# Opening of a Fourier-mixing and gated-MLP kernel: the norm row kept in its own tile, loads and weight folds in another order

## The chip, the cores and the metric

The kernel runs on one core of one Trainium2 chip. A core has TensorE (matmuls; PE in the profile, with its weight loads as PEld), VectorE (DVE), ScalarE (ACT), GpSimd (POOL) and SyncE (SP), which here only issues transfers; 16 DMA engines move data between DRAM and the on-chip memories (SBUF, and PSUM, which matmuls write). Each engine works through its own instructions in order and waits on semaphores for the others. The metric is device time in microseconds (us) of one execution; the profile is of one execution, with times from its first instruction on.

## The reference

```python
def _attn_ref(x):                      # x: 8 x 3008 x 256, float32
    X = np.fft.fft(x, axis=1)
    X = np.fft.fft(X, axis=2)
    return X.real.astype(np.float32)

def _moe_ref(x, w_in, w_out):          # x: 24064 x 256, w_in: 256 x 2048, w_out: 2048 x 256
    h = x @ w_in
    g = h * np.cos(h)
    return (g @ w_out).astype(np.float32)
```

The output is `_moe_ref` of `_attn_ref(x)`, taken as 24064 rows of 256.

## The kernel before, in words

Everything is float32. The transform over 256 columns is never done on the data: it is folded into w_in. `fold_weights(e, n)` multiplies a quarter n of w_in (512 of its 2048 columns, in `wr[n]`) with a cosine (e = 0) or sine (e = 1) matrix, two matmuls into a PSUM tile `pw`, and ScalarE copies the result into `WC` or `WS`. Row 0 of `WS` is special: the sine of column 0 is nothing, so the row holds the weights of the 128th transform column instead (the "norm" row). It is used apart: `take_wn(n)` sends the row to DRAM (`wd`) and back as a column tile `wn`, whose values scale a vector `nb` that ScalarE writes into PSUM as the start value of H (`seed`, L439). After that the row has to be zero, and `clear_row` does this with a GpSimd memset (L394).

The transform over 3008 points is split into 64 x 47. For each of the 8 batches, `load_x` brings x into two tiles `xs[0]` and `xs[1]` (16 of 32 chunk columns each; a front part, a mirrored back part, and for tile 0 one middle column, each in three transfers). Eight chunks follow, four from each tile: `fold` adds and subtracts mirrored columns (for batch 0 on DVE, L237, with a small column copy on GpSimd, L244), `first_half` multiplies with a transform matrix (L260 to L270, PSUM tile `pz`), ScalarE copies the result to `zs` (L279), and `store_z` writes it to DRAM (`zd`) in two transfers, its near part (`far` = 0) and later its far part. `load_z` reads it back transposed into `z2`, and `second_half` (L315, `pb`) yields `pq`, the tokens of a group: 6 groups in a batch.

Each group takes 8 steps over d_ff. A step t has matmuls of pq with WC and WS into H (`mm1`, L470), a doubling copy on ScalarE (`act_e`, L481), h on DVE (L486), a rounding on ScalarE (L501), the fraction on DVE (L505), a sine on ScalarE (L511), products on DVE (L515, L526 to L535), and, three steps later, matmuls with w_out (`mm2`, L562) into four accumulators M. `combine_w2` (L429) prepares sums of w_out in `VX` once. All of this is software-pipelined in one loop, in which the order of every engine's instructions is the order of the calls, written out by hand. Batch 0's transform runs before the loop, the other batches' between the steps of the batch before (`transform`); `opening` lists, by step, calls that belong to the rest of the opening.

Queues: almost all transfers are issued by SP, in program order. In the opening ScalarE issues the back part and the middle column of tile 0 and one of the two near-part stores of each chunk. The transfers of SP and ScalarE share eight semaphores; a transfer waits until the one before it on its semaphore has landed, and everything behind it on that engine waits too. GpSimd's four `clear_row` memsets stand in its instruction stream between the column copies of the chunks and behind them.

PSUM has eight banks: one tagged fft, four M, three H. In the opening the chunks' `pz` use M and most of the folds use H.

Of the kernel before, what the change touches and what calls it, by code (L numbers as in the profile page):

```python
# [11 lines left out]
FP = mybir.dt.float32  # L12
AF = mybir.ActivationFunctionType
# [6 lines left out]
NDFF = 2048  # L20
N2 = 47
NJ = 24
JA = 4
STEP = 7
XR = STEP * 15 + 5
NI = 32
IP = 4
NCH = NI // IP
# [93 lines left out]
def kernel(  # L122
# [7 lines left out]
    nc = tc.nc  # L130
# [11 lines left out]
    cpool = ctx.enter_context(tc.tile_pool(name="consts", bufs=1))  # L142
# [8 lines left out]
    def load_x(b, p):  # L151
        xv = xs[p][0 : 16 * STEP].rearrange("(e g) c -> e g c", g=STEP)
        i0 = XP * p
        back = nc.sync if b or p else nc.scalar

        def load(queue, g, c0, c1, cols, **more):
            for m in range(3):
                k = 15 if m == 2 else 16
                queue.dma_start(
                    out=xv[0:k, g + m, ND * c0 : ND * c1].rearrange("e (i d) -> e i d", d=ND),  # L160
                    in_=x_r[b, 16 * m : 16 * m + k, cols],
                    **more,
                )

        load(nc.sync, 0, 0, XP, slice(i0, i0 + XP), max_dma_last_dim=2048)
        c0 = 0 if p else 1
        load(back, 3, c0, XP, slice(64 - i0 - c0, 64 - i0 - XP, -1))
        if p == 0:
            load(back, 3, 0, 1, slice(32, 33))

    LCS = cpool.tile([128, 768], FP, tag="LCS", name="LCS")
    L = LCS[:, 0:256]
# [20 lines left out]
    def load_w2(f0, f1):  # L193
        nc.sync.dma_start(
            out=w2.rearrange("p (q c) -> p q c", c=ND)[:, 2 * f0 : 2 * f1],
            in_=moe_w_out.rearrange("(q p) c -> p q c", p=128)[:, 2 * f0 : 2 * f1],
        )

    VX = cpool.tile([128, 4 * 1024], FP, tag="VX", name="VX")
    ones = cpool.tile([1, 128], FP, tag="ones", name="ones")  # L200
    xf0 = [spool.tile([128, 2 * IP * 128], FP, tag="S", bufs=2, name="xf") for _ in range(2)]
    nc.sync.dma_start(out=LCS, in_=LCS_dr.ap())
    load_w(0)
# [1 line left out]
    nc.gpsimd.memset(xs[0][0:XR, 2048:4096], 0.0)  # L205
    nc.vector.memset(VX[:, 0:512], 1.0)
    nc.vector.memset(ones, 1.0)
    for xf in xf0:
        nc.gpsimd.memset(xf[64:128], 0.0)
    nc.vector.memset(xs[1][0:XR, 0:2048], 0.0)  # L210
    nc.gpsimd.memset(xs[1][0:XR, 2048:4096], 0.0)
    load_x(0, 0)
    load_w(1)
    load_x(0, 1)
    load_w(2)
    load_bj(0, 512)
    load_w(3)
    WC = cpool.tile([128, NDFF], FP, tag="WC", name="WC")
    WS = cpool.tile([128, NDFF], FP, tag="WS", name="WS")
    wn = cpool.tile([128, 16], FP, tag="wn", name="wn")  # L220

    bank = {"fft": 1, "M": 4, "H": 3}

# [61 lines left out]
    def store_z(b, c, far):  # L285
        half, q = divmod(c, NCH // 2)
        n = NJ - JA if far else JA
        if (b, far) not in zds:
            zds[b, far] = dpool.tile([128, n * 128], FP, tag=f"zd{far}", bufs=2, name="zd")
        zd = zds[b, far].rearrange("(h e i r) (j d) -> h i (r j) e d", h=2, e=2, r=2, d=128)  # L290
        zs = zss[b, c].rearrange("(e y) (i d) -> y e i d", e=2, d=128)
        y0 = 2 * JA if far else 0
        for e in range(2):
            queue = nc.scalar if e and b == 0 and not far else nc.sync
            queue.dma_start(
                out=zd[half, IP * q : IP * q + IP, :, e].rearrange("i y d -> y i d"),
                in_=zs[y0 : y0 + 2 * n, e],
            )
# [72 lines left out]
    def fold_weights(e, n, tag="M"):  # L371
        W = WS if e else WC
        pw = psum("pw", tag)
        for i in range(2):
            nc.tensor.matmul(  # L375
                pw,
                lhsT=CS[i][:, 128 * e : 128 * e + 128],
                rhs=wr[n][:, 512 * i : 512 * i + 512],
                start=(i == 0),
                stop=(i == 1),  # L380
            )
        nc.scalar.copy(out=W[:, 512 * n : 512 * n + 512], in_=pw)

    def take_wn(n):
        wd = dpool.tile([1, 512], FP, tag="wd", bufs=4, name="wd")
        nc.sync.dma_start(out=wd, in_=WS[0:1, 512 * n : 512 * n + 512])
        nc.sync.dma_start(
            out=wn[:, 4 * n : 4 * n + 4], in_=wd.rearrange("o (q p) -> (o p) q", p=128)
        )
        if n:  # L390
            clear_row(n)

    def clear_row(n):
        nc.gpsimd.memset(WS[0:1, 512 * n : 512 * n + 512], 0.0)  # L394

    def fold_rest(n):
        fold_weights(0, n)
        take_wn(n)

    class Step:  # L400
        pass
# [45 lines left out]
    def fill_first(s):  # L447
        s.H = psum("H", "H")
        nc.vector.memset(s.H[:, 0 : 2 * s.T], 0.25)

    def seed_first(s):
        T = s.T
        s.pq, s.nb = ready[s.b, s.grp]
        for u in range(2):
            nc.tensor.matmul(
                s.H[:, u * T : u * T + T],
                lhsT=WS[0:1, 128 * u : 128 * u + 128],
                rhs=s.pq[0:1, T : 2 * T],
                start=False,
                stop=True,  # L460
                skip_group_check=True,
            )
        clear_row(0)

    def mm1(s, e):
        T = s.T
# [218 lines left out]
    for c in range(NCH):  # L685
        if c + 1 < NCH:
            chunk(c + 1)
        first_half(0, c)
        store_z(0, c, 0)
        if c == 3:  # L690
            take_wn(0)
            fold_weights(1, 1, "H")
            fold_weights(0, 1, "H")
            take_wn(1)
    fold_weights(1, 2, "H")
    fold_weights(0, 2, "H")
    load_z(0, 0)
    load_w2(0, 4)
    take_wn(2)
    load_w2(4, 8)  # L700
    load_bj(512, 1024)
    for c in range(NCH):
        store_z(0, c, 1)
    fill_first(steps[0])
    combine_w2(0, 2)
    combine_w2(2, 4)
    second_half(0, 0)
    seed_first(steps[0])
# [21 lines left out]
    for t in range(n + LAG + 1):  # L730
        cur, prev, old, done = step(t), step(t - 1), step(t - 2), step(t - LAG)
        if cur:
            if t % per == 0:
                todo = transform(cur.b + 1) if cur.b + 1 < NB else {}
            mm1(cur, 0)
            act_e(cur)
            if t == 0:
                spread_norm()
                fold_weights(1, 3)
        if t - LAG - 1 == n - 1:  # L740
            combine_last(steps[n - 1])
            break
# [69 lines left out]
```

## Time and profile before

| | us |
|---|---|
| median of 3 runs (lowest, highest) | 1979.83 (1978.18, 1982.1) |
| the profiled execution's own time | 1979.56 |
| its span, first to last instruction | 1977.7 |
| TensorE busy in the span | 1944.8 |
| VectorE busy | 1858.2 |
| ScalarE busy | 1481.9 |
| GpSimd busy | 467.0 |

In rows of the timeline stand the start, the time taken, engine, line, operation, tile written <- tile read, count, and in brackets the idle time of the engine just before and what ended it. SPq and ACTq rows are issues of transfers. In the chain of waits each row is a start, a length and what the last-ending chain was in. "Clock" is the share of full speed that TensorE was granted.

### The profile page before, as it was taken

How to read it: one execution, taken by the hardware profiler on the slowest of the kernel's cores; microseconds unless marked ns; L12 is line 12 of the kernel's file. 1: busy time of each engine (PE TensorE's matmuls, PEld its weight loads, DVE VectorE, ACT ScalarE, POOL GpSimd, SP SyncE). 2: the span in 40 equal slices, each digit the busy share in tenths (PEclk: the TensorE clock that was granted, in tenths of full speed). 3: DMA queues.
4: the chain of work that ended last, by engine and by line, in shares of the span. 5: the costliest groups of instructions: out<-in, count | busy, mean ns of one | idle time of the engine just before them, and what ended most of it. 6: DMA issues, size and time to landing. Idle time of an engine off the chain costs nothing.

```text
span 1977.7 us, 28617 instructions
## 1 busy us (share of the span) xinstructions
PE 1944.8 (98%) x9312; PEld 1697.4 (86%) x9312; DVE 1858.2 (94%) x3211; ACT 1481.9 (75%) x2682; POOL 467.0 (24%) x430
## 2 busy tenths in 40 slices
PE   6999999999999999999999999999999999999998
PEld 3888899888988889888898888988889888898887
DVE  3999989999899998999989999999999999899998
ACT  2777777777777778777877777777777777778775
POOL 2132213331133212323122222123311223112111
PEclk8999999999999999999999999999999999999999
DMA  5421121211202112021121201211012100200000
GB/s 161 129 59 27 38 63 34 51 32 52 58 16 58 25 51 58 20 59 24 49 57 25 54 23 53 59 50 28 19 57 60 53 20 20 63 22 10 18 16 22
DMA packets 159954, 88.65 MB, mean 45 GB/s; under 512 B 104843, under 2 KB 150202, under 8 KB 158654
## 3 DMA queue, kind: packets, MB, share of 16 engines
q1 hardware_dynamic: 158480, 85.79, 16.7%
q8 instruction: 75, 1.23, 0.2%
q10 hardware_dynamic: 1326, 1.03, 0.2%
q14 instruction: 73, 0.60, 0.1%
HBM read 49.51 MB, written 37.28 MB: 44 GB/s over the span
## 4 chain that ended last, share of the span: by engine, by line
PE 91%; DVE 5%; DMA 2%; issue 1%; ACT 1%; SPq 0%; POOL 0%; DVEq 0%; ACTq 0%; POOLq 0%
PE M L562 53%; PE H L470 31%; PE pz L263 3%; PE pb L315 2%; DVE r L515 1%; DMA out_dram<-ob 1%; DVE S L535 1%; DVE S L533 1%; DVE S L526 1%; DVE r L505 1%; DVE h L486 1%; DMA xp<-in_x_dram 0%; PE pw L375 0%; DVE ob L654 0%; ACT r L501 0%
## 5 line engine op out<-in xcount | busy, mean ns | idle before, releaser
L511 ACT ACTIVATE r<-r 128x1024 f32<-128x1024 f32 (+1 forms) x384 | 398.5, 1038 | 302.5 <-DVE r L505 301.5
L562 PE MATMUL M<-S,VX 128*128 128x256 f32 (+1 forms) x2304 | 612.3, 375 | 0.0
L562 PEld LDWEIGHTS M<-S,VX 128*128 128x128 f32 x2304 | 437.8, 190 | 49.9
L470 PE MATMUL H<-pq,WS 128*128 128x256 f32 (+1 forms) x1536 | 390.0, 376 | 10.4 <-ACT ew L481 9.9
L470 PE MATMUL H<-pq,WC 128*128 128x256 f32 (+1 forms) x1536 | 393.7, 379 | 0.5 <-ACT H L439 0.5
L562 PE MATMUL M<-r,w 128*128 128x256 f32 (+1 forms) x1536 | 387.7, 375 | 0.0
L439 ACT ACTIVATE H<-nb,wn 128x256 f32<-128x256 f32 (+1 forms) x766 | 363.2, 474 | 16.2 <-DVE r L515 3.7
L470 PEld LDWEIGHTS H<-pq,WS 128*128 128x128 f32 x1536 | 289.4, 190 | 53.0 <-ACT ew L481 18.6
L486 DVE TENSOR_TENSOR h<-ew,H 128x512 f32<-128x512 f32 (+1 forms) x384 | 257.4, 670 | 80.8 <-PE H L470 72.3
L562 PEld LDWEIGHTS M<-r,w 128*128 128x128 f32 x1536 | 300.6, 196 | 27.0
L505 DVE SCALAR_TENSOR_TENSOR r<-r,h 128x512 f32<-128x512 f32 (+1 forms) x384 | 310.6, 809 | 0.0
L470 PEld LDWEIGHTS H<-pq,WC 128*128 128x128 f32 x1536 | 283.2, 190 | 29.3 <-ACT H L439 0.8
L237 POOL TENSOR_TENSOR xf<-xp 110x508 f32<-110x508 f32 x112 | 165.0, 1495 | 558.2 <-PE pz L270 541.7
L526 DVE TENSOR_TENSOR S<-r 128x512 f32<-128x512 f32 (+1 forms) x384 | 291.3, 759 | 0.1
L515 DVE SCALAR_TENSOR_TENSOR r<-h,r 128x512 f32<-128x512 f32 (+1 forms) x384 | 273.3, 712 | 0.0
L501 ACT ACTIVATE r<-H 128x512 f32<-128x512 f32 (+1 forms) x384 | 222.9, 580 | 58.2 <-DVE h L486 55.3
L481 ACT ACTIVATE ew<-H 128x512 f32<-128x512 f32 (+1 forms) x384 | 225.6, 588 | 48.9 <-PE H L470 45.4
L505 DVE SCALAR_TENSOR_TENSOR r<-r,H 128x512 f32<-128x512 f32 (+1 forms) x384 | 255.9, 667 | 0.0
L515 DVE SCALAR_TENSOR_TENSOR r<-H,r 128x512 f32<-128x512 f32 (+1 forms) x384 | 254.8, 664 | 0.3 <-ACT r L511 0.3
L501 ACT ACTIVATE r<-h 128x512 f32<-128x512 f32 (+1 forms) x384 | 236.2, 615 | 0.0
L562 PE MATMUL M<-S,w 128*128 128x256 f32 (+1 forms) x768 | 225.2, 375 | 0.0
L562 PE MATMUL M<-r,VX 128*128 128x256 f32 (+1 forms) x768 | 225.0, 375 | 0.0
(72 smaller groups left out, 1497.2 us busy)
## 6 DMA issues: line engine op xcount, KB each, us to landing
out_dram<-ob SPq DMA_DIRECT2D x728, 32.0 KB
xp<-in_x_dram SPq DMA_DIRECT2D x48, 256.0 KB
zd<-zs SPq DMA_DIRECT2D x128, 80.0 KB
z<-zd SPq DMA_DIRECT2D x8, 1280.0 KB
xp<-in_x_dram SPq DMA_DIRECT2D x38, 240.0 KB
nb<-nd SPq DMA_DIRECT2D x40, 128.0 KB
wr<-in_moe_w_in_dram SPq DMA_DIRECT2D x4, 512.0 KB
z<-zd SPq DMA_DIRECT2D x8, 256.0 KB
```

What stands on the lines that cost most here:

```text
L237: (nc.gpsimd if b else nc.vector).tensor_tensor(out=fv[:, e, :, 1:128], in0=xv[:, :, 1:128], in1=xv[:, :, 255:128:-1], op=ALU.subtract if ...
L263: nc.tensor.matmul(pz[rows, a:512], lhsT=w, rhs=fv[:, e, a:512], start=True, stop=True)
L439: nc.scalar.activation(out=s.H[:, u * T : u * T + T], in_=s.nb[:, 0:T], func=AF.Copy, bias=0.25, scale=wn[:, f : f + 1],)
L470: nc.tensor.matmul(s.H[:, u * T : u * T + T], lhsT=W[:, 128 * f : 128 * f + 128], rhs=s.pq[:, e * T : e * T + T], start=False, stop=True, ...
L481: nc.scalar.mul(out=s.ew[:, 0 : 2 * s.T], in_=s.H[:, 0 : 2 * s.T], mul=2.0)
L486: nc.vector.tensor_tensor(out=s.h[:, 0 : 2 * T].rearrange("p (u t) -> p u t", u=2)[:, :, ::-1], in0=s.ew[:, 0 : 2 * T].rearrange("p (u t) ...
L501: nc.scalar.activation(out=r, in_=h, func=AF.Copy, bias=BIG, scale=1.0)
L505: nc.vector.scalar_tensor_tensor(out=r, in0=r, scalar=-BIG, in1=h, op0=ALU.add, op1=ALU.subtract)
L511: nc.scalar.activation(out=r, in_=r, func=AF.Sin, bias=0.0, scale=SIN_SCALE)
L515: nc.vector.scalar_tensor_tensor(out=r, in0=h, scalar=-0.25, in1=r, op0=ALU.add, op1=ALU.mult)
L526: nc.vector.tensor_tensor(out=sv[:, 0:2], in0=gv[:, 2:3].to_broadcast([128, 2, T]), in1=gv[:, 0:4:3], op=ALU.subtract,)
L562: nc.tensor.matmul(acc[key][m // 2][:, 256 * (m % 2) : 256 * (m % 2) + T], lhsT=w, rhs=a, start=first, stop=s.fp == 7, skip_group_check=True,)
```

## The change

The norm row gets a tile of its own. `fold_weights(1, n)` now writes `WS` with a ScalarE activation that multiplies by a column `mask` (0 in row 0, 1 elsewhere), and DVE copies row 0 of the PSUM tile to `nrow`. `clear_row` is gone. `take_wn` is cut in two: `send_wn(n)` writes the row from `nrow` to DRAM, `take_wn(n)` reads the column back, with other work on the queue between them. The first step's seed matmul reads `nrow`.

The loads: the three transfers of the middle column of tile 0 for batch 0 go from ScalarE's queue to GpSimd's. The memset of all of tile 1 is DVE's; GpSimd's two memsets of `xf` come after its transfers. Tile 1 is loaded right after tile 0, ahead of w_in's second quarter; w_in's third and fourth quarters and w_out are issued later, between the stores. Near-part stores of batch 0's chunks 4 to 7 are both issued by ScalarE. The far-part stores are spread over the opening and steps 0 and 1, and the far load of z and the last part of BJ come in step 2.

The folds: of w_in's second quarter both after the eight chunks; the third's sine part before `second_half` and its cosine part in step 0; the fourth's in steps 1 and 2 (`early`). They use the M banks. The third `combine_w2` comes before `second_half`, the fourth in step 0.

```diff
         if p == 0:
-            load(back, 3, 0, 1, slice(32, 33))
+            load(nc.sync if b else nc.gpsimd, 3, 0, 1, slice(32, 33))
...
+    mask = cpool.tile([128, 1], FP, tag="mask", name="mask")
...
+    nc.vector.memset(mask, 1.0)
+    nc.vector.memset(mask[0:1], 0.0)
+    nc.vector.memset(xs[1][0:XR], 0.0)
+    load_x(0, 0)
     for xf in xf0:
         nc.gpsimd.memset(xf[64:128], 0.0)
-    nc.vector.memset(xs[1][0:XR, 0:2048], 0.0)
-    nc.gpsimd.memset(xs[1][0:XR, 2048:4096], 0.0)
-    load_x(0, 0)
+    load_x(0, 1)
     load_w(1)
-    load_x(0, 1)
-    load_w(2)
     load_bj(0, 512)
-    load_w(3)
...
+    nrow = cpool.tile([1, NDFF], FP, tag="nrow", name="nrow")
...
-            queue = nc.scalar if e and b == 0 and not far else nc.sync
+            queue = nc.scalar if b == 0 and not far and (e or c > 3) else nc.sync
...
-        nc.scalar.copy(out=W[:, 512 * n : 512 * n + 512], in_=pw)
+        cols = slice(512 * n, 512 * n + 512)
+        if e:
+            nc.scalar.activation(
+                out=W[:, cols], in_=pw, func=AF.Copy, bias=0.0, scale=mask[:, 0:1]
+            )
+            nc.vector.tensor_copy(out=nrow[:, cols], in_=pw[0:1, :])
+        else:
+            nc.scalar.copy(out=W[:, cols], in_=pw)
+
+    wds = {}
+
+    def send_wn(n):
+        wds[n] = dpool.tile([1, 512], FP, tag="wd", bufs=4, name="wd")
+        nc.sync.dma_start(out=wds[n], in_=nrow[:, 512 * n : 512 * n + 512])
...
-        if n:
-            clear_row(n)
-
-    def clear_row(n):
-        nc.gpsimd.memset(WS[0:1, 512 * n : 512 * n + 512], 0.0)
...
-                lhsT=WS[0:1, 128 * u : 128 * u + 128],
+                lhsT=nrow[:, 128 * u : 128 * u + 128],
...
         if c == 3:
-            take_wn(0)
-            fold_weights(1, 1, "H")
-            fold_weights(0, 1, "H")
-            take_wn(1)
-    fold_weights(1, 2, "H")
-    fold_weights(0, 2, "H")
+            load_w(2)
+            load_w2(0, 4)
+            send_wn(0)
     load_z(0, 0)
-    load_w2(0, 4)
-    take_wn(2)
     load_w2(4, 8)
+    take_wn(0)
+    load_w(3)
+    fill_first(steps[0])
+    fold_weights(1, 1)
+    fold_weights(0, 1)
+    send_wn(1)
     load_bj(512, 1024)
-    for c in range(NCH):
-        store_z(0, c, 1)
-    fill_first(steps[0])
     combine_w2(0, 2)
     combine_w2(2, 4)
+    fold_weights(1, 2)
+    take_wn(1)
+    send_wn(2)
+    combine_w2(4, 6)
+    for c in range(NCH // 2):
+        store_z(0, c, 1)
     second_half(0, 0)
     seed_first(steps[0])
+    early = {0: (0, 2), 1: (1, 3), 2: (0, 3)}
     opening = {
-        0: (
-            (fold_rest, 3),
-            (load_z, 0, 1),
-            (load_bj, 1024, NJ * 128),
-            (combine_w2, 4, 6),
-        ),
-        1: ((combine_w2, 6, 8),),
+        0: ((combine_w2, 6, 8), (take_wn, 2)) + tuple((store_z, 0, c, 1) for c in (4, 5)),
+        1: ((send_wn, 3),) + tuple((store_z, 0, c, 1) for c in (6, 7)) + ((take_wn, 3),),
+        2: ((load_z, 0, 1), (load_bj, 1024, NJ * 128)),
...
-                fold_weights(1, 3)
+            if t in early:
+                fold_weights(*early[t])
```

More of the change, by code (lines that the diff above doesn't have):

```diff
@@ L381, in fold_weights @@
             )
-        nc.scalar.copy(out=W[:, 512 * n : 512 * n + 512], in_=pw)
+        cols = slice(512 * n, 512 * n + 512)
[10 more added lines that the diff above has]
+        nc.sync.dma_start(out=wds[n], in_=nrow[:, 512 * n : 512 * n + 512])
     def take_wn(n):
-        wd = dpool.tile([1, 512], FP, tag="wd", bufs=4, name="wd")
-        nc.sync.dma_start(out=wd, in_=WS[0:1, 512 * n : 512 * n + 512])
         nc.sync.dma_start(
-            out=wn[:, 4 * n : 4 * n + 4], in_=wd.rearrange("o (q p) -> (o p) q", p=128)
+            out=wn[:, 4 * n : 4 * n + 4], in_=wds[n].rearrange("o (q p) -> (o p) q", p=128)
         )
-        if n:
-            clear_row(n)
-    def clear_row(n):
[L394 to L398, printed above, removed]
     class Step:
@@ L462, in seed_first @@
             )
-        clear_row(0)
     def mm1(s, e):
```

## The prediction

> **What bounds the kernel now.** I read the page first, then the chain of waits in order of time, then the timeline of single engines where that chain leaves TensorE.
>
> ```profile
> span 1977.7 us, 28617 instructions
> PE 1944.8 (98%) x9312; PEld 1697.4 (86%) x9312; DVE 1858.2 (94%) x3211; ACT 1481.9 (75%) x2682; POOL 467.0 (24%) x430
> PEclk8999999999999999999999999999999999999999
> ```
>
> TensorE is busy for 98% of the span, and only the first of the 40 slices (49 us) shows a lower clock. The change touches nothing behind the first steps, so all it can win or lose lies in the opening. Its chain of waits:
>
> ```profile
> 13.52 0.84 POOL xf L244 x2
> ...
> 20.79 3.63 PE pw L375 x8
> 24.42 1.01 PE pz L263 x4
> ...
> 29.12 1.61 DMA wd<-WS
> ...
> 36.88 0.59 ACT zs L279
> ...
> 37.50 1.66 DMA zd<-zs
> ...
> 39.24 2.50 DMA z<-zd
> ...
> 41.78 1.17 PE pb L315 x8
> ...
> 46.31 3.61 PE pw L375 x4
> ...
> 61.59 0.45 ACT ew L481
> ...
> 62.08 1.03 PE H L470 x4
> ```
>
> From 62.08 on the chain stays on TensorE. What is moved ahead of that point comes off the total one for one, as long as the loads behind it keep up. The largest hole is a norm row's way to DRAM (29.12):
>
> ```profile
> 30.85 0.51 POOL L394 MEMSET WS<- 1x512 f32 x1 [7.40 <-DMA wd<-WS]
> 31.56 2.82 PE L263 MATMUL pz<-xf,LCS 128*64 128x512 f32 x5 [6.07 <-POOL xf L244]
> ```
>
> GpSimd waits 7.40 us to clear the row, because the transfer that reads it must land first. Behind this memset stand GpSimd's column copies for chunks 5 to 7, so TensorE stands still for 6.07 us. The clock granted falls with it:
>
> ```profile
> 15.60:19.00 3.40, 3.40 (x15) 1.74 (x15) 2.54 (x5) 0.97 (x2) 0.74 (x2) 0.50 0.60 192
> 29.20:36.00 6.80, 4.44 (x15) 1.91 (x16) 1.72 (x3) 0.98 (x2) 1.32 (x4) 0.50 0.11 8
> 46.30:49.70 3.40, 3.40 (x5) 1.45 (x5) 2.20 (x7) 0.37 (x2) 0.00 (x0) 0.50 0.62 169
> ```
>
> (Columns: stretch, its length, busy time and count of PE, PEld, DVE, ACT, POOL, then clock, DMA share, GB/s.) Three stretches ran at half clock, each after TensorE had been idle.
>
> **The change, part by part.**
>
> *Middle column and load order.*
>
> ```profile
> 3.09 5.38 ACTq L159 DMA_DIRECT2D xp<-in_x_dram  x6
> 4.04 1.76 DVE L210 MEMSET xp<- 110x2048 f32 x1 [0.38 <-issue]
> 4.49 1.81 POOL L211 MEMSET xp<- 110x2048 f32 x1
> 9.56 1.63 SPq L159 DMA_DIRECT2D xp<-in_x_dram  x2
> 13.24 0.88 SPq L159 DMA_DIRECT2D xp<-in_x_dram  x1
> 13.60 3.68 DVE L237 TENSOR_TENSOR xf<-xp 110x508 f32<-110x508 f32 x6 [7.79 <-DMA xp<-in_x_dram]
> ```
>
> Each transfer waits for the one before it on its semaphore (eight serve SP and ACT). In the program before, the second issue of the pair at 9.56 needs the last front transfer of tile 0, and the issue at 13.24 needs the last of the three middle-column transfers. So the large loads were in by about 10.6, and the small ones (16 KB, issued last on ACT) only at 13.2; the first fold started at 13.60. GpSimd can issue them from about 3.1. No row shows a transfer from GpSimd. Below, the first fold is bounded by the large loads (10.7). The nearest price of the small ones is ACT's own: six issues took 5.38, so three 2.7, and from the last issue's end (8.5) to the last landing (13.2) it was 4.7; from 3.1 that gives 10.5, just before the large loads are in. Above stands 13.6 (no gain), and rival 1 beyond it. I take 11.3, near the lower end, because ACT's back loads have still to finish. Gain 2.3. ScalarE loses three issues, GpSimd does its two memsets behind its own; DVE clears all of tile 1, so L210 doubles to some 3.5 us and, with two tiny mask memsets ahead, ends at about 7.8, before tile 1's first load could be of use.
>
> *Tile 1.*
>
> ```profile
> 16.69 0.58 ACT L279 COPY zs<-pz 128x512 f32<-128x512 f32 x1 [5.22 <-PE pz L270]
> 17.31 0.34 ACTq L295 DMA_DIRECT2D zd<-zs  x1
> 18.83 0.86 SPq L159 DMA_DIRECT2D xp<-in_x_dram  x1
> 22.70 2.48 DVE L237 TENSOR_TENSOR xf<-xp 110x508 f32<-110x508 f32 x4 [3.26 <-PE pw L375]
> ```
>
> Tile 1's last transfer went out 1.52 us after chunk 0's store, whose semaphore it shares, and chunk 4's fold began 3.87 us after that. In the changed program it again shares the semaphore of chunk 0's store. So w_in's second quarter, moved behind it, does not bring chunk 4 forward; only the 2.3 us do: 20.4. The issues behind it on SP (w_in, BJ, four stores, w_in, w_out) stand behind it and are not in its way.
>
> *Row copy for row clearing, folds moved.* GpSimd's four memsets (0.51 each) go. Fold 1 no longer stands in front of chunk 4 (3.63), and nothing holds chunks 5 to 7. From 20.4: 0.9 to the first matmul (as 13.52 to 14.4), four chunks of about 1.25 (two folds of 0.65 on DVE), so chunk 7 is done at 26.3 at full clock. TensorE stands idle for some 3 us ahead of chunk 4 (chunk 3 ends at 20.79 less 2.3, chunk 4 starts at 21.3), so I add 0.7, about a third of what half clock took from chunks 5 to 7 (31.56 to 36.86). Chunk 7's copy then starts at 27.0 instead of 36.88: 9.9 earlier.
>
> *Stores on ScalarE.* From chunk 4 both halves of a store go out from ScalarE: 0.27 more each, the last on the path. They wait for loads as well (w_in's third quarter for chunk 6's), which goes out at about 21 and, with 1.8 us for 0.5 MB at the 295 GB/s below and z's 2.5 us of way, is in at 25.3. The w_out half now ahead of z runs beside the last store; I take 2.1 for its landing (1.66 alone, 2.5 at most, like z). z goes out at 27.0 + 0.6 + 0.3 + 2.1 = 30.0, lands at 32.5, and pb starts at 32.6 instead of 41.78: **9.2 earlier**. Fold 1 and fold 2's first half (1.8 a half, as 3.63 for two) fit between chunk 7 and pb.
>
> *The first steps.*
>
> ```profile
> 40.11 0.43 SPq L386 DMA_DIRECT2D wd<-WS  x1
> 44.89 0.36 SPq L387 DMA_DIRECT2D wn<-wd  x1
> 45.30 1.11 SPq L194 DMA_DIRECT2D w<-in_moe_w_out_dram  x1
> ...
> 46.24 3.68 PE L375 MATMUL pw<-wr,LCS 128*128 128x512 f32 x4
> 49.96 0.58 ACT L382 COPY WS<-pw 128x512 f32<-128x512 f32 x1 [3.26 <-PE pw L375]
> 50.79 0.62 DVE L486 TENSOR_TENSOR h<-ew,H 128x450 f32<-128x450 f32 x1 [2.23 <-PE H L470]
> 52.03 0.77 DVE L429 TENSOR_TENSOR VX<-w 128x256 f32<-128x256 f32 x2 [0.61 <-DMA w<-in_moe_w_out_dram]
> 53.51 0.62 DVE L505 SCALAR_TENSOR_TENSOR r<-r,H 128x450 f32<-128x450 f32 x1
> ```
>
> One fold half still stands between the first step's two matmul pairs (46.24). At half clock it took 3.68; with TensorE fed up to pb it may run at full clock, 1.8 less. Against it, fold (1,3) now lies in step 1, and its row copy stands on DVE ahead of the fraction (L505): TensorE 1.8, ScalarE 0.6, DVE about 0.5 (L394's 0.51 is nearest), some 1.9 later relative to h than before. Fold (0,3) in step 2 costs a copy of 0.58 on ScalarE that step 1 had before. The last combine, 1.5 of DVE, moves to where DVE waits, and w_out's second half, a little after z, goes out at 30.4 and needs the 6.7 us it took here (45.30 to 52.03): 37.1, and two combines later (1.5) DVE is free at 38.6, before h needs it near 40. These nearly cancel (-1.8 to +1.9); I take 0.1 of gain. The mask's multiply adds some 0.1 to each of four copies, inside these bounds.
>
> *Behind it.*
>
> ```profile
> 59.18 0.35 SPq L304 DMA_DIRECT2D z<-zd  x1
> 72.46 1.05 PE L315 MATMUL pb<-BJ,z 128*128 128x128 f32 x8
> ```
>
> The rest of z goes out after all far stores and two norm transfers, by my count at 50.6 (twenty issues of 0.43, as at 40.11, from 41 on, and 1 for the last landing), 8.6 earlier; its user (72.46) comes 9.3 earlier and had 13.3 us, of which it keeps 12.6. Nothing is lost there.
>
> Sum against the profiled execution: 1979.56 - 9.2 - 0.1 = **1970.3 us**. That execution lies 0.3 under the median of the runs (1979.83), so no correction is made.
>
> **Rivals.**
>
> 1. *The middle column comes late from GpSimd.* DVE's long memset (to 7.8) holds GpSimd off, and the three issues (2.7) with their way to landing (4.7) come after it: the fold starts at 15.2, 3.9 later than I take, and all that follows with it: 1974.2. For it: no GpSimd transfer has a row. Against: the memsets of the two engines (L210 and L211 above) ran beside each other here at 1.76 and 1.81. The Trainium skill ("SBUF — State Buffer", SBUF: two separate sides) says that GpSimd cannot write the descriptors of its transfers while DVE runs an operation in a two-port mode; by that rule, were the memset such an operation, this rival would come true, and no run here shows which it is.
>
> 2. *The clock stays low.* Half clock followed each time TensorE stood idle (6.07 us before the second stretch). TensorE will idle some 3 us ahead of chunk 4 and a little around pb. If both bring a half-clock stretch, chunks 5 to 7 take 1.3 more than I put in, and the first step's fold the 1.8 that I set against the later row copy: 1973.4. The Trainium skill ("TensorE: Matmul & The Clock Gate", Part 1: The HAM clock gate) says that one idle window of about 3.4 us is enough for half rate and one busy one for full. The trace agrees: its half-clock stretches are 3.4 and 6.8 us long.
>
> 3. *A new wait on norm values.* On SP the second row's transfer stands behind z, w_out (1 MB) and w_in (0.5 MB), as the one at 40.11 stood behind w_out, where its follower went out 4.8 later.
>
> ```profile
> 3.00:13.50 10.50, 7.26 (x10) 2.58 (x10) 2.38 (x3) 2.64 (x4) 3.24 (x3) 1.00 1.03 295
> ```
>
> At these 295 GB/s the 1.8 MB take 6.2 us from 31.5 on; with 2.5 of way (z's) for the row, and 2.5 for the column that follows it, wn has it at 42.7; step 2's seed asks for it at about 44. At the 170 to 190 GB/s of the half-clock stretches' rows it takes 3.3 to 4.4 more and is 2 to 3 late: 1972.3 to 1973.3.
>
> 4. *The holes only move* (the change does not do what it says): chunk 6's or 7's store waits on ScalarE for w_in, and z for w_out, 5 us or more: 1975.5 to 1981.
>
> 5. *Slower.* GpSimd's queue is so slow that the middle column lands after 24.5, 13 us later than I take. That is the point where the gain is spent; at 28 it is 1987. Against: it has 47 KB to move.
>
> **How the numbers follow.** A measurement here tells about 0.2%, 4 us (the runs differ by 1978.18 to 1982.1): faster is below 1975.9. Chances: forecast 0.50 (1966.5 to 1972), late column 0.12, clock 0.13, norm wait 0.10, holes that move 0.10 (0.09 of it within 4 us, 0.01 slower), slower queue 0.05. So faster 0.85, same 0.09, slower 0.06. Range 1966 to 1976: the good ends of the terms (fold 0.6, no slow clock at the chunks 0.7, store 0.4, first steps 1.8) give 1966.8; the first three rivals lie inside; 0.15 above is left out.
>
> **What would show it.** Right: no wait of GpSimd on wd; the first fold near 11.3; chunk 4's near 20.4; no stop of TensorE between chunks 4 and 7; z's near load issued near 30, pb at 32.6; TensorE without holes from about 52.8. Wrong: a first fold after 13.6; ScalarE standing at a store's issue for more than 2 us; seeds (L442) waiting for wn; z's near load after 34.

## The result

| | median us | runs | ratio to the kernel before | 95% interval |
|---|---|---|---|---|
| before | 1980.57 (1977.15 to 1985.10) | 20 | | |
| after | 1977.10 (1972.27 to 1979.21) | 20 | 0.9981 | 0.9974 to 0.9988 |

The change gains some 3.5 us, 0.19%, where 9.3 were predicted; the interval leaves out 1, so there is a gain, but it is smaller than the 4 us that the prediction called the least a measurement here can tell. The profiled execution took 1977.74, 1.82 less than that of before. Its page, then its chain of waits (start, length, what the last-ending chain was in):

```profile
span 1976.0 us, 28616 instructions
PE 1946.9 (99%) x9312; PEld 1699.4 (86%) x9312; DVE 1864.0 (94%) x3217; ACT 1482.3 (75%) x2682; POOL 467.2 (24%) x428
PEclk8999999999999999999999999999999999999999
```

```profile
9.77 4.37 DMA xp<-in_x_dram
...
17.36 2.37 DMA zd<-zs
19.75 4.03 DMA xp<-in_x_dram
...
28.03 4.99 DMA zd<-zs
...
33.41 1.52 DMA zd<-zs
...
35.05 2.80 DMA z<-zd
...
37.89 1.17 PE pb L316 x8
...
44.25 3.34 PE pw L376 x4
...
52.59 0.68 DVE nrow L388
...
60.57 0.96 PE H L472 x4
```

The norm row's way to DRAM (wd) is gone from it. In its place stand transfers of x up to 23.8 and a store of 4.99 us, the one of chunk 4. pb starts 3.9 earlier than before, not 9.2, and half of that is lost behind it: the fold between the first step's matmuls (44.25) takes 3.34, nearly the 3.61 of before. The rows of the timeline at the marks that the prediction named:

```profile
3.32 1.69 POOL L159 DMA_DIRECT2D xp<-in_x_dram  x3 [0.77 <-DVE xp L205]
...
14.11 4.87 DVE L238 TENSOR_TENSOR xf<-xp 110x508 f32<-110x508 f32 x8 [1.75 <-DMA xp<-in_x_dram]
...
23.96 2.48 DVE L238 TENSOR_TENSOR xf<-xp 110x508 f32<-110x508 f32 x4 [4.97 <-issue]
...
32.00 0.58 ACT L280 COPY zs<-pz 128x512 f32<-128x512 f32 x1 [0.69 <-DMA zd<-zs]
...
48.44 0.62 DVE L488 TENSOR_TENSOR h<-ew,H 128x450 f32<-128x450 f32 x1 [5.51 <-PE H L472]
```

And the stretches of the granted clock (third number from the end; the first after the comma is TensorE's busy time):

```profile
23.20:30.00 6.80, 5.21 (x15) 2.44 (x16) 5.14 (x8) 1.17 (x2) 2.28 (x4) 0.50 0.85 260
...
36.80:40.20 3.40, 1.70 (x11) 1.30 (x11) 1.85 (x5) 1.38 (x3) 0.00 (x0) 1.00 1.03 348
40.20:47.10 6.90, 6.90 (x14) 3.59 (x13) 1.52 (x4) 0.89 (x2) 0.00 (x0) 0.51 0.69 199
```

Two stretches of 6.8 us at half clock: one on chunks 4 to 6, one from the first seed nearly to the end of that fold.

### The profile page after: what moved, and what is told of

It reads as the page before. It is cut to its first block, busy times and chain, and to the rows that moved or that the text cites. A ratio compares the mean times of both kernels' runs of the same rounds, so it can differ in the third digit from the quotient of the medians.

```text
span 1976.0 us, 28616 instructions
## 1 busy us (share of the span) xinstructions
PE 1946.9 (99%) x9312; PEld 1699.4 (86%) x9312; DVE 1864.0 (94%) x3217; ACT 1482.3 (75%) x2682; POOL 467.2 (24%) x428
## 4 chain that ended last, share of the span: by engine, by line
PE 91%; DVE 5%; DMA 2%; ACT 1%; issue 1%; SPq 0%; POOL 0%; DVEq 0%; ACTq 0%; POOLq 0%
PE M L564 53%; PE H L472 31%; PE pz L264 3%; PE pb L316 2%; DVE r L517 1%; DMA xp<-in_x_dram 1%; DVE S L537 1%; DMA out_dram<-ob 1%; DVE S L535 1%; DVE r L507 1%; DVE S L528 1%; DMA zd<-zs 0%; DVE h L488 0%; DVE ob L656 0%; ACT r L513 0%
```

## The experiments

Times are compared with the kernel before on the same chip at the same time (its medians were 1979.3 to 1981.35). All ratios are below; the readings follow.

| run | median us | minus before | ratio | 95% interval |
|---|---|---|---|---|
| same_again | 1976.03 | -3.6 | 0.9980 | 0.9970 to 0.9989 |
| mid_on_scalar | 1978.55 | -1.1 | 0.9988 | 0.9979 to 0.9998 |
| before_mid_on_gpsimd | 1980.41 | +0.8 | 1.0006 | 0.9997 to 1.0014 |
| before_norm_row_copy | 1979.24 | -0.4 | 0.9999 | 0.9990 to 1.0008 |
| busy_before_chunk4 | 1976.48 | -3.7 | 0.9979 | 0.9971 to 0.9988 |
| busy_around_pb | 1975.64 | -4.5 | 0.9973 | 0.9963 to 0.9984 |
| tile1_back_on_gpsimd | 1974.43 | -5.8 | 0.9971 | 0.9959 to 0.9982 |
| w_out_behind_z | 1974.51 | -5.7 | 0.9967 | 0.9955 to 0.9978 |
| fill_around_pb | 1973.36 | -5.9 | 0.9970 | 0.9959 to 0.9980 |
| fold4_later | 1979.23 | -0.1 | 1.0000 | 0.9991 to 1.0008 |
| loads_decoupled | 1971.09 | -8.2 | 0.9965 | 0.9951 to 0.9979 |
| all_together | 1975.06 | -4.2 | 0.9979 | 0.9971 to 0.9988 |
| before_filled | 1978.51 | -2.8 | 0.9988 | 0.9979 to 0.9997 |
| filled_and_w_out_behind_z | 1972.80 | -8.6 | 0.9955 | 0.9943 to 0.9968 |
| decoupled_filled | 1970.28 | -11.1 | 0.9944 | 0.9932 to 0.9957 |
| decoupled_filled_sums_later | 1970.45 | -10.9 | 0.9944 | 0.9931 to 0.9958 |
| one_row_filling | 1977.06 | -2.7 | 0.9983 | 0.9973 to 0.9993 |
| fourth_quarter_first | 1972.07 | -7.7 | 0.9956 | 0.9944 to 0.9968 |

### Is one profile of the opening the opening?

> The changed kernel once more, nothing edited, as a second look at its opening. If the late arrival of the large loads (first fold 14.1) belongs to the program, the first fold starts again between 13.9 and 14.4, z's near load goes out between 34.6 and 35.5 and pb starts between 37.4 and 38.4. If it is chance of one execution, the first fold starts anywhere from 11.3 to 14, and what follows moves with it by the same amount. Time 1977 to 1978 in the first case.

The same program, profiled again, took 1973.19, 4.6 less than the first profile. First the timeline, then the clock of this second execution:

```profile
12.43 4.87 DVE L238 TENSOR_TENSOR xf<-xp 110x508 f32<-110x508 f32 x8 [1.88 <-DMA xp<-in_x_dram]
```

```profile
23.50:26.90 3.40, 3.40 (x14) 1.20 (x11) 2.84 (x5) 0.59 (x1) 0.54 (x1) 0.51 0.59 144
...
37.10:40.50 3.40, 3.13 (x12) 2.04 (x13) 1.52 (x4) 1.11 (x3) 0.00 (x0) 1.00 0.93 310
40.50:43.90 3.40, 3.40 (x7) 1.78 (x6) 0.00 (x0) 0.85 (x2) 0.00 (x0) 0.50 0.50 118
```

Of the 4.6, 1.7 is the arrival of tile 0, 0.4 the way from there to chunk 4's fold, 0.4 the way on to pb and 1.5 the way from pb to step 0's h; on the last two half clock lasts 3.4 instead of 6.8. The remaining 0.5 comes in step 1. So neither expectation held: the late first fold was chance in part, and chance does not end with the loads. In the nine profiles of kernels that load tile 0 as the changed one does, the first fold starts at 12.0 to 14.2, median 12.6; in the three that load as before, at 13.6 to 14.5. The 14.11 of the first profile is thus a bad draw, and 11.3 was never reached. From here on a single profile stands for the order of waits, and medians for the time.

### The middle column

```diff
-            load(nc.sync if b else nc.gpsimd, 3, 0, 1, slice(32, 33))
+            load(nc.sync if b else nc.scalar, 3, 0, 1, slice(32, 33))
```

> The changed kernel with the three middle-column transfers back on ScalarE's queue. Theory A (a GpSimd queue beside the others slows the large loads): w_in's first quarter lands near 5.5 instead of 7.0, the large transfers of tile 0 are in by 10.6 to 11.2, the small ones last at about 13.2, so the first fold is at 13.6, 0.5 earlier, and the time is 0 to 0.7 lower. Theory B (the large loads are late for another reason): they are as late as before, 13.9, the small ones behind them at about 15.5, the first fold at 15.5 to 16 and the time 1 to 2 higher.

The first fold started at 13.36 and the column landed last, at 13.1, nearly as theory A had it; but the time rose, as theory B had it, with a median 2.5 above same_again's. So neither theory holds as a whole. In same_again GpSimd's queue was in use, and w_in's first fold was still 1.8 earlier than in the first profile (its row copy at 9.87 instead of 11.68), so the late w_in of the first profile is not owed to that queue. That GpSimd's transfers cost the large loads nothing does not follow: by the semaphore events of the traces ScalarE's last large load landed at 11.2 to 11.9 in the four profiles with the column on ScalarE, and at 11.8 to 14.0, median 12.3, in the fifteen of the changed kernel and its variants with the column on GpSimd. That is some 0.7 later; no run tells whether the queue or the order of the loads does it. In sum the move seems worth something, not less than nothing as theory A said, though the intervals of the two runs meet. The other way round, in the kernel before:

```diff
-            load(back, 3, 0, 1, slice(32, 33))
+            load(nc.sync if b else nc.gpsimd, 3, 0, 1, slice(32, 33))
```

> The kernel before with one part of the change alone: the three middle-column transfers from GpSimd. Theory A (a GpSimd queue beside the others slows the large loads): the small transfers are in by 11.3 but the large ones only at 13 to 14, the first fold starts at 13 to 14.3 and the time is within 1 of before. The prediction's view (the small transfers alone were late): the first fold at 11.3, and up to 2.3 off the time, less what chunk 4 waits for tile 1.

```profile
4.50 1.81 POOL xp L211
6.31 1.11 POOL xp L159 x2
7.42 6.39 DMA xp<-in_x_dram
```

In this chain GpSimd issues only at 6.3, behind its memsets, and the column lands at 13.8; the first fold starts at 14.18. First fold and time lie where theory A had them, but the column was again what came last: ScalarE's large loads were in at 12.2. Alone the move gains nothing (+0.8). The change also takes a memset off GpSimd and puts two behind the issues, and there the column is in by 11.0 (first profile).

### The row copy alone

`take_wn` and the first seed read `nrow` instead of `WS`, the mask is multiplied in as in the change, and

```diff
-        if n:
-            clear_row(n)
...
-        clear_row(0)
```

> The kernel before with the mask and the row copy alone: GpSimd clears no row, folds, loads and stores stay where they were. My theory: GpSimd's wait of 7.40 and TensorE's stop of 6.07 go, chunk 7's copy starts at 31 to 32 instead of 36.9, the third fold fills part of the way of z, pb starts at 36 to 37.5, and the time is 3 to 5 lower. Rival (the hole only moves): another wait of SP's queue ahead of z's near load, of 3 or more, takes its place, pb starts after 40 and the time is within 1 of before.

The holes went as my theory said: chunk 7's copy started at 31.9 and pb, in the chain, 4.4 earlier than before, although the first fold was 0.9 later in this profile (14.46). But the median is 0.4 lower only.

```profile
37.38 1.17 PE pb L319 x8
...
42.86 3.71 PE pw L379 x4
```

From pb to step 0's h it took 10.6, against 9.0 before, with 6.8 us of half clock instead of 3.4 (the fold: 3.71). So 1.6 of the 4.4 is lost there without any new wait, which made the clock the first suspect. It does not account for the whole: this profile took 1977.61, 1.6 under its own median.

### The clock

Ahead of chunk 4, then around pb:

```diff
+        if c == 4:
+            keep_busy(10, "H", 512)
         first_half(0, c)
```

> The changed kernel with ten matmuls of 512 columns on constant data (4.3 us at full clock, their result used by nothing) ahead of chunk 4, where TensorE is idle for 3.5 to 5 while tile 1 arrives. Theory C (the clock is halved because TensorE idles there): the half-clock stretch of 3.4 or 6.8 that begins near 23 is gone, from chunk 4's fold to chunk 7's copy it takes 6 to 6.8 instead of 7.7 and 8.0, and the time falls by 0.8 to 1.7. Rival D (what chunks 5 to 7 lose is ScalarE's wait at a store's issue): that distance stays at 7.5 or more at full clock, ScalarE stands for 1 to 2 at chunk 6's or 7's store, and the time stays within 0.5.

```profile
18.06 8.78 PE pd L413 x20
26.84 1.01 PE pz L264 x5
...
32.74 1.51 DMA zd<-zs
```

I had sized it wrongly: a matmul of 512 columns is two records of 0.44, so the ten took 8.8 and held chunk 4 up to 26.84, some 4 longer than its data. Yet chunk 7's copy (31.81) came no later than in the first profile, since chunks 4 to 7 then ran at full clock with no wait (26.84 to 31.81, 5.0; in same_again 22.7 to 29.6, 6.9), and stores landed in 1.5. The time stayed at -3.7: what the filling cost, clock and stores gave back. The run does not decide between theory C and rival D, since the half clock and the long landings of the stores are both gone from it, and the time stayed within 0.5 as rival D said.

```diff
+    keep_busy(3, "M", 512)
     second_half(0, 0)
+    keep_busy(2, "M", 384)
     seed_first(steps[0])
```

> The changed kernel with three matmuls of 512 columns ahead of pb and two of 384 behind it (1.3 and 0.65 us at full clock, results used by nothing), where TensorE idles for the load of z and for ScalarE's copy. Theory C (the clock is halved by the idle time around pb): the half-clock stretch that begins near 40 is gone in the profile or falls to one window of 3.4, from pb to step 0's h it takes 7.3 to 8 instead of 9.0 and 10.6, and the time falls by 1 to 2.5. Rival E (norm values come next): step 1's or 2's seeds then wait for wn, h of step 2 stays where it was and the time stays within 0.7.

Measured against the kernel before, the time lies 0.9 under same_again's. From pb to h 7.6 and no half clock there; but the filling read w_out's sums, waited for them and held pb up by 2. So it was made smaller and read the transform matrices (`fill_clock` is `keep_busy` on `LCS`):

```diff
+    fill_clock(1, "M", 512)
     second_half(0, 0)
+    fill_clock(1, "M", 512)
     seed_first(steps[0])
```

> The changed kernel with less filling around pb than before: one matmul of 512 columns ahead of pb and one behind it (0.87 each at full clock), on the transform matrices, which are there from the start, so that nothing is waited for. The first filling cost 2 ahead of pb because it read w_out's sums. Theory C (clock): pb starts right after z lands, from pb to step 0's h it takes 7.5 to 8.3 instead of 9.0 to 11.7, at most one window of half clock there, and the time is 1973.5 to 1975.5. Rival G (such a short filling does not hold the clock): the distance stays above 9 and the time at 1976 to 1977.

In its chain and its windows:

```profile
36.90 1.16 PE pb L316 x8
38.06 0.86 PE pd L424 x2
...
41.43 1.93 PE pw L376 x4
```

```profile
37.40:40.90 3.50, 3.50 (x17) 2.14 (x17) 0.66 (x2) 0.70 (x3) 0.00 (x0) 1.00 1.01 336
40.90:44.30 3.40, 3.21 (x10) 1.62 (x10) 0.95 (x4) 1.81 (x4) 0.00 (x0) 1.00 0.49 133
```

The fold takes 1.93 instead of 3.34, pb to h 7.3 instead of 9.0 to 10.6. The median lies 2.7 under same_again, 2.3 measured against the kernel before. Rival G falls, and theory C stands in so far as the clock is the cause; whether idle time is what lowers it was asked with the same two matmuls on one row (one partition of both operands instead of 128, which takes TensorE as long):

```diff
-                pd[:, 0:n], lhsT=LCS[:, 0:128], rhs=LCS[:, 0:n], start=i == 0, stop=i == k - 1
+                pd[:, 0:n], lhsT=LCS[0:1, 0:128], rhs=LCS[0:1, 0:n], start=i == 0, stop=i == k - 1
```

> The run fill_around_pb (1973.4, 5.9 under the kernel before on its chip) with the same two matmuls on one row instead of 128, so that TensorE is busy for as long and the array is not. If idle time alone lowers the clock, all is as in that run: from pb to step 0's h 7.3 to 7.8, time 5 to 7 under the kernel before. If matmuls of one row do not count as activity, the half-clock window behind pb is back: 9 to 11 from pb to h, time 2.5 to 4 under the kernel before.

```profile
36.79:40.20 3.41, 2.35 (x12) 1.63 (x13) 1.15 (x3) 0.70 (x2) 0.00 (x0) 1.00 0.96 338
40.20:43.61 3.41, 3.41 (x9) 2.18 (x8) 1.52 (x4) 0.40 (x1) 0.00 (x0) 0.50 0.78 255
```

TensorE was busy for 2.35 of 3.41, 1.2 of it on one row, and half clock followed; pb to h took 10.6 and the time is that of the changed kernel. Matmuls on one row did not hold the clock. The first seed and the spreading of the norm (`seed_first`, `spread_norm`) are such matmuls, and they fill much of the window in question. In the kernel before, too, the stretch ahead of the last half clock is a busy one:

```profile
42.87:46.28 3.41, 2.59 (x12) 1.67 (x11) 0.74 (x3) 1.20 (x3) 0.97 (x2) 1.00 0.53 170
```

Of these 2.59, only 1.14 are matmuls of more than one row. Lastly, the same filling in the kernel before:

> The kernel before with the short filling of TensorE ahead of and behind pb. If the half clock around pb belongs to both kernels alike, it gains here what it gained in the changed kernel, 2.5 to 4, and the time is 1975.5 to 1977.5. If the kernel before loses little there (one half-clock window in its profile against two in the changed kernel's), the time is 1978 to 1980.

The time lies in the second range, because the kernel before was slow on this chip (1981.35); the gain, 2.8 (0.6 to 4.2), is what the filling gained in the changed kernel too (2.3). In the profile pb was 0.6 later than in that of before and pb to h took 7.3 instead of 9.0. So the change did not bring the loss around pb; both kernels have it.

### Stores, w_out and tile 1

```diff
             load_w(2)
-            load_w2(0, 4)
             send_wn(0)
     load_z(0, 0)
+    load_w2(0, 4)
```

> The changed kernel with the first half of w_out (1 MB) issued behind z's near load, as in the kernel before, instead of ahead of the stores of chunks 4 to 7. If that load is what makes chunk 4's store take 4.9 to 5 to land (ScalarE stands at chunk 7's store until then, z's near load waits too): the store lands in 2 to 3, z's near load goes out 2.1 to 2.6 after chunk 7's copy instead of 3.05 and 3.12, and pb is 0.5 to 1.2 earlier. Against it: w_out's sums on DVE start near 40 instead of 35, and would hold up step 0's h if they ran past 44. Time between 1 lower and 1 higher.

```profile
31.32 1.53 DMA zd<-zs
32.90 2.95 DMA z<-zd
35.90 1.17 PE pb L316 x8
```

No store of chunks 4 to 7 stands in the chain with more than 1.53; z goes out 2.5 after chunk 7's copy (30.39), and pb is 5.5 after it instead of 5.8 and 5.9. From chunk 4's fold to pb the profile is 0.5 to 0.9 shorter, while the median, measured against the kernel before, is 2.1 under same_again's (the intervals overlap); where the rest comes from is not shown. The chain shows no wait for w_out's sums. Then tile 1:

```diff
-        back = nc.sync if b or p else nc.scalar
+        back = nc.sync if b else nc.gpsimd if p else nc.scalar
```

> The changed kernel with tile 1's three back transfers issued by GpSimd behind the middle column, so that none of them shares a semaphore with chunk 0's store. My theory (the shared semaphore holds tile 1 up): tile 1 is in by 17 to 18.5, chunk 4's fold starts at 19 to 20.5 right behind chunk 3 instead of 21.9 and 24.0, TensorE is idle for less than 1.5 there, no half-clock stretch begins near 23, chunk 7's copy is at 26 to 28, and the time falls by 1.5 to 3.5. Rival F (GpSimd's transfers take the engines from tile 0): the first fold starts 1 to 2 later and eats it up, the time stays within 0.7.

Chunk 4's fold started at 18.71, 6.2 behind the first fold instead of 9.2 to 9.9: the shared semaphore held it, as the prediction had it, and the transfers from GpSimd cost tile 0 nothing (first fold 12.48). Rival F falls. Two new waits took part of it:

```profile
24.41 2.80 ACTq L296 DMA_DIRECT2D zd<-zs  x2
27.25 0.59 ACT L280 COPY zs<-pz 128x512 f32<-128x512 f32 x1 [2.87 <-DMA wr<-in_moe_w_in_dram]
```

```profile
34.50:37.90 3.40, 2.58 (x9) 1.65 (x8) 0.30 (x1) 0.70 (x2) 0.00 (x0) 0.50 1.07 340
37.90:41.30 3.40, 3.40 (x7) 1.99 (x8) 1.22 (x4) 0.89 (x2) 0.00 (x0) 0.50 0.49 130
```

ScalarE stands for 2.2 at chunk 6's store, whose semaphore w_in's third quarter holds, and behind pb half clock lasts three windows, to 44.7. Tile 1's edit once more, now with w_in's third quarter ahead of the stores and all of w_out behind the first norm column:

```diff
     load_bj(0, 512)
+    load_w(2)
...
         if c == 3:
-            load_w(2)
-            load_w2(0, 4)
             send_wn(0)
     load_z(0, 0)
+    take_wn(0)
+    load_w2(0, 4)
     load_w2(4, 8)
-    take_wn(0)
     load_w(3)
```

> The changed kernel with tile 1's back transfers on GpSimd, w_in's third quarter issued ahead of the stores, and both halves of w_out behind z's near load and the first norm column. My theory (transfers sharing a semaphore or the engines with the stores make up most of what the prediction missed): chunk 4's fold at 18 to 19.5, chunk 7's copy at 24 to 26, z's near load out at 26.5 to 28.5, pb at 29.5 to 31.5, no ScalarE wait over 0.7 at a store's issue. If the clock then stays full around pb the time is 1968 to 1971, with two or three half-clock windows there, as in the run with tile 1 alone, 1970.5 to 1974. Rival I (what is won by pb is lost again to norm values or w_out's sums): h of step 2 not before 53 and the time above 1973.

1971.09: chunk 4's fold at 18.2, chunk 7's copy at 25.1, z out at 27.7, pb at 30.4, one window of half clock. Rival I falls, since the norm column was in time; w_out's sums ended just as h could start (40.66).

### The folds and the sum

```diff
-    early = {0: (0, 2), 1: (1, 3), 2: (0, 3)}
+    early = {0: (0, 2), 2: (1, 3), 3: (0, 3)}
```

> The changed kernel with the fold of w_in's fourth quarter in steps 2 and 3 instead of 1 and 2 (its row's way to DRAM and back one step later too). My theory (the row copy and the mask copy ahead of step 1's fraction are on the path): from step 0's h to step 1's 4.1 to 4.7 instead of 5.3 to 5.8, to step 3's 12.9 to 13.2 instead of 13.2 to 13.7, and the time falls by 0.3 to 0.8. Rival H (the copies cost the same wherever they stand): step 2 or 3 becomes longer by as much, the sum to step 3 stays at 13.2 to 13.7 and the time within 0.3.

My theory fell, and the result is worse than H had it: measured against the kernel before, this is 3.5 slower than same_again. From step 0's h to step 1's it took 3.3 (5.8 in the changed kernel), but to step 2's then 6.8 (4.1) and to step 3's 5.5 (3.8). Both folds stand in the chain, and one of them met half clock; that TensorE has no hole left for them in steps 2 and 3 is the likely reason, not a shown one:

```profile
51.57 1.73 PE pw L376 x4
...
57.51 3.21 PE pw L376 x4
```

The next run has that edit as well, beside the loads of loads_decoupled and the filling of fill_around_pb, and is worse than the loads alone:

> All edits at once: the loads as in the run decoupled, the short filling on both sides of pb, the fourth fold in steps 2 and 3. If the causes add up (loads and semaphores 3 to 5, clock 1.5 to 3, fold 0.3 to 0.8, from 1976.5): 1967.5 to 1971.5, pb at 29.5 to 31.5, at most one half-clock window behind it, step 3's h at 50 to 53. If they are the same microseconds counted twice: 1971.5 to 1974.

1975.06 lies outside both ranges. pb came at 31.4 as expected, but from step 0's h to step 3's it took 15.3, against 12.3 in loads_decoupled.

> The run loads_decoupled (1971.1) with the short filling around pb, the fourth fold where the change put it. If the later fold was what spoilt the run with everything together, this one is at 1968 to 1970. If w_out's sums on DVE hold step 0's h (they ended at 40.7 and 42.1 in the two runs, just ahead of h), the filling brings nothing: 1970.5 to 1972.5, h at 40.5 to 42.

Without the later fold it is 1970.28, faster than both kernels by the intervals, and no half clock is left in its profile behind the first fold. Measured against the kernel before it lies 2.9 under the loads alone (the intervals overlap), but its profile hardly differs from theirs (h at 40.49 and 40.66), since the next wait is there:

```profile
29.16 9.84 DMA w<-in_moe_w_out_dram
39.02 1.11 DVE VX L440 x3
...
40.49 0.63 DVE h L496
```

w_out's second half lands at 39.0, its sums stand ahead of h on DVE. They were moved, and then w_in's fourth quarter was put ahead of that half:

```diff
-    combine_w2(4, 6)
...
-        0: ((combine_w2, 6, 8), (take_wn, 2))
+        0: ((combine_w2, 4, 6), (combine_w2, 6, 8), (take_wn, 2))
```

> The run decoupled_filled with w_out's third sums on DVE behind step 0's h instead of ahead of it. If these sums are the next wait, h of step 0 comes 1.5 to 3 earlier than in that run, at 38 to 39.5, and the time is 1 to 2.5 lower, 1967.5 to 1969.5. If not, it is the same within 0.7.

> The run decoupled_filled_sums_later with w_in's fourth quarter issued ahead of w_out's second half instead of behind it. In that run the fourth quarter landed at 41.1 and step 1's fold waited for it. If that was the last wait, the fold starts at 39.5 to 40, frac of step 0 comes 1 to 1.5 earlier, and the time is 1 to 1.5 lower. If w_out's second half, now landing at 41 or later, holds step 0's fraction on DVE instead, the time is the same within 0.7.

The last of their chains' transfers, of the one and of the other:

```profile
30.29 10.77 DMA wr<-in_moe_w_in_dram
41.20 1.97 PE pw L377 x4
```

```profile
30.52 10.61 DMA w<-in_moe_w_out_dram
41.15 1.11 DVE VX L440 x3
```

With the sums later, h came at 39.4 as expected, and nothing was won. With the fourth quarter first the median is 1.6 higher, 3.2 measured against the kernel before (the intervals overlap), not 1 to 1.5 lower. Whichever of the two transfers is last, it lands at 41.1, and a step of the opening needs it: the arrival of the 2.5 MB of weights issued behind z is the wait that is left in these runs. That no other order of loads would do better is not shown.

The two edits that answer what the prediction missed, in the changed kernel (with w_out's sums behind h):

> The changed kernel with the short filling around pb, the first half of w_out behind z's near load, and w_out's third sums on DVE behind step 0's h instead of ahead of it. If clock and w_out are two separate losses, they add up: 3 and 2 off 1976.5, 1970.5 to 1972.5, which leaves the prediction 1 for the first fold. If they overlap: 1972.5 to 1974.

8.6 under the kernel before, 4.9 more than the change alone, where 2.3 and 2.1 were found singly. In its chain the norm column is the next wait:

```profile
33.57 9.02 DMA wn<-wd
42.67 0.46 ACT H L449
```

## Why the prediction was wrong

| step | predicted | first profile | second (same_again) | what the runs showed |
|---|---|---|---|---|
| first fold | 11.3 | 14.11 | 12.43 | median 12.6 of nine |
| to chunk 4's fold | 9.1 | 9.9 | 9.5 | 6.2 without the shared semaphore |
| to chunk 7's copy | 6.6 | 8.0 | 7.7 | 6.9 in loads_decoupled, at full clock |
| to z's near load | 3.0 | 3.1 | 3.1 | 2.5 with w_out behind it |
| to pb | 2.6 | 2.8 | 2.7 | |
| to step 0's h | about 7.2 | 10.6 | 9.0 | 7.3 with filling |
| to step 3's h | some 15 | 13.7 | 13.2 | 13.0 before |

(The predicted 7.2 is the 9.0 of before less the 1.8 for full clock; 15 is the 13.0 of before and the 1.9. The differences from the predicted column add up to 7.4 and 2.9, which is what the two profiled executions lie above 1970.3.)

*Middle column and load order.* The mechanism was right: three issues took 1.69 and the column was in by 11. The term was mis-sized. "So the large loads were in by about 10.6" read the landing of the last front load; the last of ScalarE's back loads landed at 11.2 in that profile and at 12.3 in the median with the column on GpSimd. With the small ones out of the way the first fold waits for it, to 12.6 in the median. Gain about 1.5 (medians of the profiles), not 2.3. Rival 1 fell: GpSimd issued from 3.32, and DVE's long memset began only at 4.62.

*Tile 1.* Right: it came 9.2 to 9.9 behind the first fold, where 9.1 was taken; taken off the shared semaphore, chunk 4's fold comes some 3 earlier, and the time falls by 2.1.

*Row copy.* The wait of GpSimd and the stop of 6.07 went, as said. "I add 0.7" for the clock was too little: 3.4 to 6.8 us ran at half clock while TensorE's idle time ahead of chunk 4 was 4.62 in the first profile. And a stop was missed: "the w_out half now ahead of z runs beside the last store" priced one store at 2.1. That store took 1.52, but chunk 4's took 4.99 beside 1.5 MB of weights, and chunk 7's, on its semaphore, waited for it. This is rival 4 in small, 0.5 to 0.9 by the profile and not 5.

*The first steps.* This is the step that failed most: "with TensorE fed up to pb it may run at full clock, 1.8 less". It ran at half clock for 3.4 to 6.8, because what counts comes after: pb, ScalarE's copy, and two sets of one-row matmuls. The prediction's "each after TensorE had been idle" hides that ahead of the third half-clock stretch of before TensorE was idle for only 0.8 of 3.41 and busy for 2.59. The filling returned 2.3 to 2.7. The term against it, 1.9 for the row copy, was too high in turn; 0.3 to 0.8 is left of it at step 3, and moving it away cost 3.5. In the second profile these two errors cancel (9.0 + 13.2 from pb to step 3's h, where 7.2 + 15 were taken): there the sum is right by luck.

*Behind it.* z's far part went out at 52.6 and 57.2, not at 50.6, and nobody waited for it (its user started at 71.05).

*Rivals.* Rival 2 is what happened, priced at 1973.4 because first fold and stores were taken as forecast. Rival 3 does not show in the first profile. In the second the way of the second norm row is in the chain:

```profile
34.78 5.50 DMA wd<-nrow
```

It is level with the fold there, as the seed that reads the column began at 43.53 with no idle time of ScalarE ahead of it. It becomes the wait as soon as the other two losses are mended (the 9.02 above). Rival 5 fell.

The account in medians: 9.3 predicted, 3.5 measured, 5.8 missing. Clock around pb and w_out beside the stores, mended together, return 4.9; the first fold is 1.3 later than taken, and the row copy costs 1.1 to 1.6 less. That is 4.6 to 5.1 of the 5.8, which closes the account within the intervals (1.8 to 2.8 on each side for a single run). The half clock at chunks 4 to 7 goes with the idle time ahead of chunk 4: of the changed kernel and its variants, eight of the nine profiles with chunk 4 late and nothing put ahead of it show it, and none of the six with tile 1's back transfers on GpSimd. Not settled is what it cost beside the waits for stores, since the one run on it held the chunk up as well.

## What to carry to other kernels

A gain that removes a hole in the opening has to be followed to the next arrival of data: here a store beside weight loads, then the clock, then the norm column, then the weights themselves. Put large loads that are not needed yet behind the small transfers on the path, and see which transfer each one's semaphore makes it wait for. Where TensorE waits or runs one-row matmuls for some microseconds ahead of dense work, two unneeded matmuls on all rows were cheaper here than a window at half clock (1.7 us of work, 2.3 to 2.8 won). Take two profiles of an opening before sizing a term by tenths.

## What was not expected of the hardware

*The clock.* Half clock comes in windows of 3.41 us on a grid that lies differently in each execution (behind the idle time ahead of chunk 4 it began at 23.2, 23.5, 22.8 and 23.8 in four profiles). The Trainium skill ("TensorE: Matmul & The Clock Gate", Part 1: The HAM clock gate) says that the window is free-running and that this makes the cold time vary between runs; the traces agree. In two executions of one program the half clock of the opening lasted 13.7 and 6.8 us, and the ways on which it differed make up some 2 of the 4.6 us between them. Its section "HAM oscillation — how this bites in real kernels" states the rule as no idle gap over some 3.4 us. Here the measurement differs: half clock followed a window in which TensorE was busy for 3.13 of 3.40 (same_again), and one with 2.35 of 3.41, half of it one-row matmuls (one_row_filling), and did not follow when the filling had 128 rows. The longest gaps of TensorE around pb in these two were 1.07 and 1.94. What separates the windows is matmuls of more than one row: on this grid, in the first 75 us of the 20 profiles, TensorE was busy with them for at most 1.69 of 3.41 us in the 34 full-clock windows that half clock followed, and for at least 1.43 in the 316 that full clock followed. With one-row matmuls counted the first go up to 3.15.

*Small stores beside large loads.* A store of 16 KB landed in 1.5 alone and in 4.9 to 5.7 with 1.5 MB of weights in flight (28.03 4.99 above). The Trainium skill ("DMA: Bandwidth & Descriptors", Issuing engines are not separate DMA queues) says that transfers of all issuing engines interleave on the same 16 DMA engines; the trace agrees in so far as ScalarE's stores land late beside SyncE's loads.
